# Gathering softmax probabilities by 4 wide matmuls and a block transpose in a decode-attention kernel

## The chip, the cores and the metric

The kernel runs on one core of one Trainium2 chip. The metric is the device time of one execution, in microseconds (us); lower is better. The kernel before took 1296.13 to 1296.85 us in its 25 executions.

## The reference, cut to what matters

One token is decoded for 4 sequences: a layer norm, attention over a cache of 8192 keys for each of 32 heads, a gated feed-forward layer, two residual sums. Nearly all bytes are the caches `k_cache` and `v_cache`, each (4, 32, 8192, 128) in bf16, 537 MB together.

```python
def _A_ref(x, k_cache, v_cache, wq, wo):
    q = (x @ wq).reshape(B, Sq, H, Dh).transpose(0, 2, 1, 3)
    scores = jnp.einsum("bhqd,bhkd->bhqk", q, k_cache) * (Dh ** -0.5)
    p = _softmax(scores, axis=-1)
    o = jnp.einsum("bhqk,bhkd->bhqd", p, v_cache)
    return o.transpose(0, 2, 1, 3).reshape(B, Sq, H * Dh) @ wo
```

## The kernel before

K and V come in loads of 4 MB (two heads each) into a ring of 4 slots of SBUF. VectorE (DVE) transposes K blocks, TensorE (PE) makes the scores, and eight heads form a group: 16 groups in all. At the end of a group ScalarE (ACT) takes the exponential of 128 x 512 scores into `E_sb`. There the keys run along the columns; this kernel's value matmuls take them from the partitions (weights of 128 x 32 out of `PTz`). The kernel before moves them with 64 small matmuls per group: each takes 32 columns of `E_sb` as the stationary operand and a selection matrix `Sel` as the moving one. Two ACT copies then place the result in `PTz`, the stationary operand of the value matmuls.

```python
        def chain_pt(g):
            def f(e):
                mm = None
                for rr in range(16):
                    for a in range(4):
                        mm = e.matmul(bP[g % 2][32 * a:32 * (a + 1), 32 * rr:32 * rr + 32],
                                      E_sb[:, 32 * rr:32 * rr + 32], Sel[:, a, :], start=True, stop=True,
                                      tile_position=(0, 32 * a))
                return mm
            pt_of[g] = P("pe", f, [exp_of[g], c_sel] + list(ptc_of.get(g - 2, ())))
            # ... two ACT copies: PTz <- bP[g % 2], strided, lists them in ptc_of[g]
```

The scores of one head and its value product, 16 matmuls each, are the bulk of PE's program (cut):

```python
        def pe_score(s):
            # ...
                for v in range(4):
                    l0 = LQ0 + (t * 4 + v) * 32 - 4 * hh
                    for j in range(4):
                        # ... rhs = 512 columns of kT
                        mm = e.matmul(bS[g % 2][32 * j:32 * (j + 1), :], Lq[:, l0:l0 + 32], rhs,
                                      start=(s % GS == 0 and v == 0), stop=(s % GS == GS - 1 and v == 3),
                                      tile_position=(0, 32 * j))
```

Each `matmul` becomes two PE instructions, a weight load and a matmul (5827 of each in the trace of the kernel before).

## Time and profile before

Median 1296.3 us.

| | before |
|---|---|
| span of the profiled execution | 1294.5 us |
| read from HBM | 550.8 MB |
| busy: DVE, PE, ACT | 48%, 39%, 4% |
| PE matmuls (and as many weight loads) | 5827 |

First, from the page of the kernel before: busy time by engine, the row of the DMA engines' busy tenths in 40 slices, and the DMA queues (packets, MB, share of the 16 engines' span).

```profile
PE 499.5 (39%) x5827; PEld 193.4 (15%) x5827; DVE 625.4 (48%) x641; ACT 46.1 (4%) x102; POOL 10.6 (1%) x22
DMA  9999999999999999999999999999999999999998
q1 hardware_dynamic: 26016, 550.78, 99.5%
q8 instruction: 45, 0.74, 0.2%
q14 instruction: 7, 0.06, 0.0%
```

No compute engine is near full (DVE, the fullest, is busy 48%); the DMA engines are, at 80% or more in every slice and 90% or more in all but the last. Queue 8 brings instructions, 45 packets in the span, each of 16384 bytes in the trace. The loads are queue 1.

Second, the table by stage (start and end, length, busy time of each engine, PE clock, DMA share, GB/s), two of its rows.

```profile
140.00:400.00 260.00, 102.68 (x1187) 40.02 (x1187) 125.68 (x125) 8.54 (x20) 0.00 (x0) 0.60 1.00 430
400.00:800.00 400.00, 149.21 (x1666) 55.28 (x1665) 195.44 (x194) 10.67 (x25) 0.00 (x0) 0.60 1.00 431
```

In these stages the DMA engines moved 430 to 431 GB/s with a share of 1.00.

Third, groups of instructions that the change touches, and the largest one of DVE (busy us, mean ns of one | idle time just before them and its releaser).

```profile
L397 DVE STREAM_TRANSPOSE kT<-ring 128x1024 uint32<-128x1024 uint32 x512 | 587.9, 1209 | 578.8 <-DMA ring<-in_A_k_cache_dram 578.6
L506 ACT ACTIVATE PTz<-PS 64x512 bf16<-64x512 f32 x32 | 18.9, 592 | 16.5 <-PE PS L492 16.1
L492 PE MATMUL PS<-Sel,E_sb 128*32 128x32 bf16 x1024 | 11.0, 183 | 1.6 <-ACT E_sb L476 1.1
```

Fourth, the timeline at one group's end (start us, length us, engine, line, operation; idle before in brackets).

```profile
613.82 0.69 ACT L476 ACTIVATE E_sb<-PS,negm 128x512 bf16<-128x512 f32 x1
614.65 0.66 PE L492 MATMUL PS<-Sel,E_sb 128*32 128x32 bf16 x64
615.40 1.21 ACT L506 ACTIVATE PTz<-PS 64x512 bf16<-64x512 f32 x2 [0.81 <-PE PS L492]
619.57 9.13 DVE L397 STREAM_TRANSPOSE kT<-ring 128x1024 uint32<-128x1024 uint32 x8 [9.25 <-DMA ring<-in_A_k_cache_dram]
629.39 1.90 PE L439 MATMUL PS<-ring,PTz 128*32 128x512 bf16 x16 [2.73 <-DMA ring<-in_A_v_cache_dram]
```

The gather ends at 615.3 and `PTz` is ready at 616.6, but its first reader starts at 629.39, when its V load has landed. DVE is idle for 9.25 us until 619.57, when the next K load lands.

### The profile page before, as it was taken

The numbers are of one execution on the slowest core, as the hardware profiler recorded it, in microseconds if no ns is written. First come the engines' busy times: TensorE is split into PE (matmuls) and PEld (weight loads), VectorE is DVE, ScalarE is ACT, GpSimd is POOL, SyncE is SP. The second block draws the span as 40 slices with busy tenths as digits, with TensorE's granted clock in tenths as the row PEclk, the third lists the DMA queues.
The fourth block names the chain that finished last, engine by engine and source line by source line (L and its number), as shares of the span: only waits on it lengthen the run. The fifth ranks groups of instructions, "written<-read, shape, count | busy, mean of one in ns | idle before, by whom it ended". The sixth has DMA issues, their size and how long they took to land.

```text
span 1294.5 us, 12693 instructions
## 1 busy us (share of the span) xinstructions
PE 499.5 (39%) x5827; PEld 193.4 (15%) x5827; DVE 625.4 (48%) x641; ACT 46.1 (4%) x102; POOL 10.6 (1%) x22
## 2 busy tenths in 40 slices
PE   3444334335244244334334334343343343343436
PEld 1011111112011021111111111011110111111114
DVE  5964644535544544535535435445535446445300
ACT  2000000000000000000000000000000000000000
POOL 3000000000000000000000000000000000000000
PEclk9996565665565565565666665665665665656655
DMA  9999999999999999999999999999999999999998
GB/s 405 434 428 432 432 428 433 431 430 430 433 431 430 433 429 431 433 427 433 434 426 434 431 427 435 429 431 435 425 434 432 426 435 428 431 434 429 429 376 322
DMA packets 26076, 551.58 MB, mean 426 GB/s; under 512 B 2340, under 2 KB 8232, under 8 KB 9256
## 3 DMA queue, kind: packets, MB, share of 16 engines
q1 hardware_dynamic: 26016, 550.78, 99.5%
q8 instruction: 45, 0.74, 0.2%
q14 instruction: 7, 0.06, 0.0%
q10 hardware_dynamic: 8, 0.00, 0.0%
HBM read 550.77 MB, written 0.00 MB: 425 GB/s over the span
## 4 chain that ended last, share of the span: by engine, by line
DMA 81%; PE 12%; SPq 4%; DVE 3%; issue 0%
DMA ring<-in_A_v_cache_dram 79%; PE PS L439 7%; PE PS L415 4%; SPq L220 2%; DVE kT L397 2%; SPq L236 1%; DMA ring<-in_A_wq_dram 1%; DMA ring<-in_B_w_down_dram 1%; SPq L228 1%; SPq L256 0%; PE PS L330 0%; DVE Lq L374 0%; DVE ring L347 0%; PE PS L357 0%; PE PS L637 0%
## 5 line engine op out<-in xcount | busy, mean ns | idle before, releaser
L397 DVE STREAM_TRANSPOSE kT<-ring 128x1024 uint32<-128x1024 uint32 x512 | 587.9, 1209 | 578.8 <-DMA ring<-in_A_k_cache_dram 578.6
L415 PE MATMUL PS<-kT,Lq 128*32 128x512 bf16 x2048 | 241.6, 619 | 563.3 <-DVE kT L397 443.8
L439 PE MATMUL PS<-ring,PTz 128*32 128x512 bf16 x2048 | 215.0, 564 | 208.7 <-DMA ring<-in_A_v_cache_dram 208.3
L415 PEld LDWEIGHTS PS<-kT,Lq 128*32 128x32 bf16 x2048 | 69.4, 135 | 692.4 <-DVE kT L397 471.9
L439 PEld LDWEIGHTS PS<-ring,PTz 128*32 128x32 bf16 x2048 | 64.5, 127 | 326.4 <-DMA ring<-in_A_v_cache_dram 197.1
L474 ACT ACTIVATE negm<-PS 128x1 f32<-128x1 f32 x16 | 2.7, 171 | 1156.3 <-PE PS L470 1156.3
L511 DVE TENSOR_SCALAR Zs<-PS,rinv 128x512 f32<-128x512 f32 x16 | 11.6, 723 | 36.4 <-PE PS L439 36.4
L506 ACT ACTIVATE PTz<-PS 64x512 bf16<-64x512 f32 x32 | 18.9, 592 | 16.5 <-PE PS L492 16.1
L518 PE MATMUL PS<-SelZ,Zs 128*128 128x8 f32 x128 | 19.1, 276 | 0.9 <-DVE Zs L511 0.9
L518 PEld LDWEIGHTS PS<-SelZ,Zs 128*128 128x128 f32 x128 | 17.6, 213 | 10.6 <-issue 8.9
L453 DVE TENSOR_REDUCE mx<-PS 128x1 f32<-128x512 f32 x16 | 10.5, 658 | 5.4 <-PE PS L415 5.4
L492 PEld LDWEIGHTS PS<-Sel,E_sb 128*32 128x32 bf16 x1024 | 10.4, 96 | 8.3 <-ACT E_sb L476 7.1
L492 PE MATMUL PS<-Sel,E_sb 128*32 128x32 bf16 x1024 | 11.0, 183 | 1.6 <-ACT E_sb L476 1.1
L476 ACT ACTIVATE E_sb<-PS,negm 128x512 bf16<-128x512 f32 x16 | 11.0, 688 | 0.5
L481 PEld LDWEIGHTS PS<-sig,Gsum 128*128 128x128 f32 x32 | 7.8, 305 | 12.6 <-issue 12.6
L481 PE MATMUL PS<-sig,Gsum 128*128 128x1 f32 x32 | 9.2, 356 | 0.0
L470 PEld LDWEIGHTS PS<-onesf,rowx 1*128 1x128 f32 x32 | 7.3, 281 | 13.0 <-issue 13.0
L470 PE MATMUL PS<-onesf,rowx 1*128 1x1 f32 x32 | 8.6, 336 | 0.0
L523 DVE CAST OT<-PS 128x8 bf16<-128x8 f32 x16 | 2.1, 132 | 11.6 <-PE PS L518 11.6
L347 DVE CAST ring<-PS 128x512 bf16<-128x512 f32 x4 | 2.5, 683 | 10.0 <-PE PS L330 10.0
L485 DVE RECIPROCAL rinv<-PS 128x1 f32<-128x1 f32 x16 | 2.1, 130 | 9.3 <-PE PS L481 9.3
L330 PE MATMUL PS<-ring,xnT 128*32 128x512 bf16 x32 | 3.6, 629 | 6.6 <-DMA ring<-in_A_wq_dram 6.6
(78 smaller groups left out, 81.3 us busy)
## 6 DMA issues: line engine op xcount, KB each, us to landing
ring<-in_A_k_cache_dram SPq DMA_DIRECT2D x64, 4096.0 KB, 29.7
ring<-in_A_v_cache_dram SPq DMA_DIRECT2D x63, 4096.0 KB, 34.0
ring<-in_A_wq_dram SPq DMA_DIRECT2D x1, 4096.0 KB, 12.3
kT<-in_A_wo_dram SPq DMA_DIRECT2D x8, 512.0 KB, 17.3
ring<-in_A_v_cache_dram SPq DMA_DIRECT2D x1, 2048.0 KB, 18.5
ring<-in_A_v_cache_dram SPq DMA_DIRECT2D x2, 1024.0 KB, 18.2
ring<-in_B_w_gate_dram SPq DMA_DIRECT2D x1, 1792.0 KB, 19.9
ring<-in_B_w_up_dram SPq DMA_DIRECT2D x1, 1792.0 KB, 23.5
```

The costliest lines, as they stand in the source:

```text
L220: return [(lambda e: e.dma_start(wo_v[:, HW * t:HW * t + HW, :], A_wo.rearrange("(h p) f -> p h f", p=128)[:, HW * t:HW * t + HW, :]).then ...
L228: return e.dma_start(ringv(slot)[:, c0:c1], kv_src(t, A_v_cache)[:, c0:c1]).then_inc(s_piece[i], 16)
L236: return e.dma_start(wd_v[:, t0:t1, :], B_w_down.rearrange("(t p) f -> p t f", p=128)[:, t0:t1, :]).then_inc(s_piece[3 + i], 16)
L397: return e.transpose(kT[:, buf, i * q:(i + 1) * q].bitcast(U32), ringv(src)[:, base + i * q:base + (i + 1) * q].bitcast(U32))
L415: mm = e.matmul(bS[g % 2][32 * j:32 * (j + 1), :], Lq[:, l0:l0 + 32], rhs, start=(s % GS == 0 and v == 0), stop=(s % GS == GS - 1 and v == 3),
L439: mm = e.matmul(bO[g % 2][32 * rq:32 * (rq + 1), :], PTz[:, g % 2, l0:l0 + 32], ringv(slot)[:, r0 * 128:(r0 + 4) * 128], start=(s % GS == ...
L470: p2_of[g] = P("pe", lambda e: e.matmul(bX[:, 0:1], rowx[0:1, :], onesf[0:1, 0:1], start=True, stop=True), [d2b_of[g], c_ones])
L481: L_of[g] = P("pe", lambda e: e.matmul(bX[:, 0:1], Gsum[:, :], sig[:, 0:1], start=True, stop=True), [exp_of[g], a1_of[g], d_g])
L492: mm = e.matmul(bP[g % 2][32 * a:32 * (a + 1), 32 * rr:32 * rr + 32], E_sb[:, 32 * rr:32 * rr + 32], Sel[:, a, :], start=True, stop=True, ...
L506: return e.activation(dst, src, ACT.Copy)
L511: z_of[g] = P("dve", lambda e: e.tensor_scalar(Zs[:, :], bO[g % 2][:, :], rinv[:, g % 2:g % 2 + 1], None, op0=ALU.mult), [pv_of[g * GS + G ...
L518: mm = e.matmul(bX[:, 256:264], Zs[:, 128 * r:128 * (r + 1)], SelZ[:, r, :], start=(r == 0), stop=(r == 3))
```

## The change

The intent is to take work from PE: 4 matmuls of 512 columns with `Sel` as the stationary operand gather whole rows of `E_sb`; ACT copies the result to SBUF; one DVE instruction is meant to transpose it in blocks of 32 x 32, which is what this layout needs; the two ACT copies then read from there. The gather now writes one PSUM tile (`bP[0]`) instead of two in turn, and waits for the copy of the group before. The diff, cut:

```diff
+        Ep = SB("Ep", [128, 512], BF16)
+        Et = SB("Et", [128, 512], BF16)
@@ chain_pt
-                for rr in range(16):
-                    for a in range(4):
-                        mm = e.matmul(bP[g % 2][32 * a:32 * (a + 1), 32 * rr:32 * rr + 32],
-                                      E_sb[:, 32 * rr:32 * rr + 32], Sel[:, a, :], start=True, stop=True,
-                                      tile_position=(0, 32 * a))
+                for a in range(4):
+                    mm = e.matmul(bP[0][32 * a:32 * (a + 1), :], Sel[:, a, :], E_sb[:, :], start=True, stop=True,
+                                  tile_position=(0, 32 * a))
                 return mm
-            pt_of[g] = P("pe", f, [exp_of[g], c_sel] + list(ptc_of.get(g - 2, ())))
+            pt_of[g] = P("pe", f, [exp_of[g], c_sel, epc_of.get(g - 1)])
+            epc_of[g] = P("act", lambda e: e.activation(Ep[:, :], bP[0][:, :], ACT.Copy), [pt_of[g], et_of.get(g - 1)])
+
+        def chain_et(g):
+            et_of[g] = P("dve", lambda e: e.transpose(Et[:, :], Ep[:, :]), [epc_of[g]] + list(ptc_of.get(g - 1, ())))
 # ... the two copies into PTz
-                    src = bP[g % 2][p0:p0 + 64, :].rearrange("p (q r m) -> p q m r", q=4, r=4)
+                    src = Et[p0:p0 + 64, :].rearrange("p (q r m) -> p q m r", q=4, r=4)
 # ... chain_et(g) stands on DVE just before the key transposes of step 8 g + 10
```

More of the change, by code (lines that the diff above doesn't have):

```diff
@@ L387, in bass_sequential_preLN__mha_block_cached__glu_gated_glu__decode_kernel @@
         mx_of, d2_of, exp_of, pt_of, ptc_of, L_of, d3_of = {}, {}, {}, {}, {}, {}, {}
-        z_of, ot_of, otc_of = {}, {}, {}
+        z_of, ot_of, otc_of, epc_of, et_of = {}, {}, {}, {}, {}
         def dve_T(s):
@@ L504, in fc @@
                                   [[2 * 4128, 64], [1024, 4], [32, 32], [1, 4]])
-                    src = bP[g % 2][p0:p0 + 64, :].rearrange("p (q r m) -> p q m r", q=4, r=4)
+                    src = Et[p0:p0 + 64, :].rearrange("p (q r m) -> p q m r", q=4, r=4)
                     return e.activation(dst, src, ACT.Copy)
-                ops.append(P("act", fc, [pt_of[g], zp] + last_pv))
+                ops.append(P("act", fc, [et_of[g], zp] + last_pv))
             ptc_of[g] = ops
@@ L530, in bass_sequential_preLN__mha_block_cached__glu_gated_glu__decode_kernel @@
         for s in range(NST + LAG - 2 + 4):
+            g = hook(s, 10)
+            if g is not None:
+                chain_et(g)
             tr = dve_T(s) if s < NST else iter(())
@@ L646, in bass_sequential_preLN__mha_block_cached__glu_gated_glu__decode_kernel @@
         p_o = P("pe", lambda e: e.matmul(bP[0][0:NB, 0:128], oT[:, :], ident[:, :], start=True, stop=True),
-                [d_o] + list(ptc_of[gl]) + list(ptc_of[gl - 1]))
+                [d_o, epc_of[gl]])
         o0 = P("dve", lambda e: e.tensor_copy(o_sb[:, :], bP[0][0:NB, 0:128]), [p_o])
```

## The prediction

> **What bounds the kernel now.** The DMA engines. The table by stage gives DMA share 1.00 and 430 to 431 GB/s from 140 to 1216 us. 550.8 MB are read; at 431 GB/s that alone is 1278 of the 1294.5 us span. [...]so no compute engine can speed up the middle. The chain that ended last is 79% V loads. VectorE works 48%; its key transposes (512, 1209 ns each) wait 579 us for K loads. PE works 39%, ACT 4%.
>
> **What the change does**, once for each of 16 groups:
> - removes 64 32-column matmuls with their weight loads: 0.66 to 0.74 us a group in the timeline;
> - adds 4 matmuls of 512 columns on 4 column tiles; four such value matmuls take about 0.65 us in the timeline, so PE gains next to no time, though it issues 1920 instructions fewer (2 x 60 x 16);
> - adds an ACT copy 128x512 out of PSUM: about 0.60 us (line 346, same shape, 602 ns), 9.6 us in all;
> - adds a DVE transpose 128x512 bf16: estimated 0.6 us, half of the 1209 ns of 1024 elements, 10 us in all;
> - moves the two PTz copies (592 ns each) behind these, reading SBUF instead of PSUM; I leave them at 0.6 us.
> So exp to PTz grows from about 2.7 to about 4.2 us a group.
>
> **Is that on the critical path?** In the middle, no. At the group near 611 us: exp ends 614.5, gather would end near 615.3, copy 616.0, transpose 616.7, PTz 618. DVE idles until the K load lands at 619.57, and the group's first value matmul starts only at 629.39, after its V load. About 3 us to spare; at 146 and 1162 us 2 to 3 us.
>
> In the first group DVE is delayed: its keys have already landed, so the transposes now starting at 73.2 us wait behind the new one for exp (76.6), gather and copy: about 5.5 us later, and K and V slots are released that much later (82.2 to about 87.7, 87.6 to about 91). But loads are then issued some 29 us before they land, so about 15 us of transfers are still queued; DMA won't run dry, and the delay is absorbed at the next K load (DVE idled 9.75 us before 91.98).
>
> In the last group PTz is written by about 1233.3 instead of 1232.4; the next value matmul waits for DMA until 1236.5. Tail unchanged.
>
> A small gain: 12693 instructions came with 0.74 MB on the instruction queue, so 1900 fewer save about 0.11 MB, about 0.25 us of DMA time, an estimate.
>
> **Predicted:** 1296.1 us, 8 in 10 between 1295.2 and 1297.0. Faster by over 2%: 0.5%; within 2%: 99%; slower: 0.5%.
>
> **What would show it.** DMA share still 1.00 at 430 to 431 GB/s in the middle, and 431 from 60 to 140 us; DVE and ACT busy up by about 10 us each, PE within 2 us; about 1890 instructions fewer; DVE's idle time before the key transposes down by about 10 us or somewhat more, with a new wait of about 5 us for ACT at the first group only; fewer instruction-queue bytes.
>
> **What would make it wrong.** The new transpose or copy taking several us; DVE waiting for ACT in every group beyond the K load, so that slot releases slip by more than the queued 15 us; a hole in the DMA row at the first group; a strided PTz copy much slower from SBUF.

The sum is 1296.3 less about 0.25 us, so about 1296.1; that the middle can't be sped up by a compute engine rests on the share of 1.00 and the 1278 us of loads alone. The 15 us of queued transfers are an estimate; the trace gives about as much: 29.7 us from issue to landing (K loads, median), less the 9.7 us from one landing to the next and the 5.5 us of delay.

## The result, and the profile after

Median 1295.22 us (4 runs, 1295.11 to 1295.36) against 1296.3 us before: 1.08 us less. The ratio of the fast runs is 0.9992, with an interval of 0.9975 to 1.0009: the same, by the 2% measure. The changed kernel, run again later beside the kernel before on another occasion, gave 1295.18 against 1296.34, so the 1.1 us is real although it is small. No execution of the one overlaps one of the other.

The same lines of the page, after:

```profile
PE 494.7 (38%) x4867; PEld 183.3 (14%) x4867; DVE 636.9 (49%) x657; ACT 70.7 (5%) x118; POOL 10.7 (1%) x22
DMA  9999999999999999999999999999999999999998
q1 hardware_dynamic: 26016, 550.78, 99.5%
q8 instruction: 38, 0.62, 0.2%
q14 instruction: 7, 0.06, 0.0%
```

The table by stage, after, the same two rows:

```profile
140.00:400.00 260.00, 99.96 (x943) 36.29 (x944) 128.81 (x130) 14.68 (x24) 0.00 (x0) 0.61 1.00 431
400.00:800.00 400.00, 148.38 (x1379) 53.34 (x1382) 200.17 (x201) 18.34 (x30) 0.00 (x0) 0.59 1.00 431
```

The loads are the same. PE has 960 matmuls and 960 weight loads less, and queue 8 fetched 38 blocks instead of 45. The groups, after:

```profile
L399 DVE STREAM_TRANSPOSE kT<-ring 128x1024 uint32<-128x1024 uint32 x512 | 587.9, 1209 | 480.9 <-DMA ring<-in_A_k_cache_dram 480.9
L502 DVE STREAM_TRANSPOSE Et<-Ep 128x512 bf16<-128x512 bf16 x16 | 11.4, 712 | 97.4 <-ACT Ep L498 97.4
L511 ACT ACTIVATE PTz<-Et 64x512 bf16<-64x512 bf16 x32 | 34.0, 1062 | 12.8 <-DVE Et L502 12.5
L498 ACT ACTIVATE Ep<-PS 128x512 bf16<-128x512 f32 x16 | 9.6, 597 | 11.3 <-PE PS L494 11.3
L494 PE MATMUL PS<-E_sb,Sel 128*32 128x512 bf16 x64 | 7.0, 429 | 1.9 <-ACT E_sb L478 1.3
```

DVE now "waits 97.4 us for ACT". That is no new delay: idle time is booked to the instruction that ends it. The idle time before the key transposes is 97.9 us less (578.8 to 480.9), and the new transpose stands in that gap. The timeline of the same group shows how:

```profile
615.07 0.40 PE L494 MATMUL PS<-E_sb,Sel 128*32 128x512 bf16 x4
615.52 0.60 ACT L498 ACTIVATE Ep<-PS 128x512 bf16<-128x512 f32 x1 [0.50 <-PE PS L494]
616.15 0.71 DVE L502 STREAM_TRANSPOSE Et<-Ep 128x512 bf16<-128x512 bf16 x1 [5.74 <-ACT Ep L498]
616.90 2.15 ACT L511 ACTIVATE PTz<-Et 64x512 bf16<-64x512 bf16 x2 [0.78 <-DVE Et L502]
619.68 9.13 DVE L399 STREAM_TRANSPOSE kT<-ring 128x1024 uint32<-128x1024 uint32 x8 [2.82 <-DMA ring<-in_A_k_cache_dram]
629.50 1.90 PE L441 MATMUL PS<-ring,PTz 128*32 128x512 bf16 x16 [2.72 <-DMA ring<-in_A_v_cache_dram]
```

The idle 9.25 us became 5.74 us, the transpose of 0.71 us, and 2.82 us: the key transposes still start when their load lands.

So the new work is hidden. Where do 1.08 us come from? Not steadily from everywhere: the K and V loads land now earlier, now at the same time. A load raises its semaphore 16 times, and the trace has the time of each rise. The profile counts 16 DMA engines, and the author reads each rise as one engine's share of the load having landed, so that the time from the first to the last of the 16 is how far the latest engine is behind the earliest. That reading is not shown: the trace has the 16 rises but does not name their engines. Worked out from the recorded rises, for the loads around each jump (a load is complete at its 16th rise):

```
load (order)   before: complete, first to 16th   after: complete, first to 16th   after - before
   24th           238.00     2.17                   237.97     2.17                  -0.03
   25th           248.77     3.21                   247.68     2.17                  -1.09
   30th           297.46     3.34                   296.42     2.36                  -1.04
   31st           307.18     3.34                   307.27     3.50                  +0.09
   49th           482.41     3.70                   482.38     3.80                  -0.04
   50th           493.30     4.87                   492.09     3.81                  -1.21
   60th           590.42     4.89                   589.22     3.83                  -1.20
   61st           600.13     4.90                   600.23     5.13                  +0.10
  123rd          1205.87     8.44                  1205.54     8.43                  -0.33
  124th          1216.73     9.59                  1215.25     8.43                  -1.48

start of every eighth packet on queue 8 (the 9th, 17th, 25th, 33rd, 41st)
   before    243.1   491.1   730.6   966.5   1214.5
   after     300.4   593.4   886.3  1179.3   (38 in all, no 41st)
```

Three things can be seen. The spread of the 16 rises grows from 2 us to over 8 us during the run (by the reading, some engines fall further and further behind), and what waits for a load starts after its last rise (63rd load of the kernel before: 16th rise at 619.55 us, key transposes at 619.57). The spread doesn't grow evenly but by jumps of 1.0 to 1.3 us, with smaller ones of up to 0.6 us between. And each large jump comes in the load in flight after the 9th, 17th, 25th, 33rd, 41st instruction block. The durations of these packets repeat with a period of eight as well (changed kernel, from the 3rd block: 1060, 1099, 1107, 1095, 1016, 1026, 1073, 1078 ns, then about the same again). In the late loads 7 of the 16 rises come within 1.2 us and the rest 5 us or more after the first.

**Theory A** (a hypothesis: the trace names the engine neither of a packet nor of a rise). PE's instruction blocks go to about half of the DMA engines in turn, one block to each in eight. A block holds up its engine's share of the loads by about 1.1 us (the packets listed above took 1.02 to 1.11 us). The time is set by the engine that is furthest behind, and it gets one more block at every eighth. The kernel before meets five such blocks, the changed one four: one step of about 1.1 us.

**Theory B.** The gain comes from the new route itself: less PE time or PSUM traffic, `PTz` read from SBUF, other waits.

**The plain share of bytes** (as predicted): 7 blocks of 16384 bytes are 0.115 MB, and at 431 GB/s that is about 0.3 us.

### The profile page after: what moved, and what is told of

Its sections match the earlier page's. It is cut to its first block, busy times and chain, and to the rows that moved or that the text cites. A ratio compares the mean times of both kernels' runs of the same rounds, so it can differ in the third digit from the quotient of the medians.

```text
span 1293.4 us, 10805 instructions
## 1 busy us (share of the span) xinstructions
PE 494.7 (38%) x4867; PEld 183.3 (14%) x4867; DVE 636.9 (49%) x657; ACT 70.7 (5%) x118; POOL 10.7 (1%) x22
## 4 chain that ended last, share of the span: by engine, by line
DMA 80%; PE 12%; SPq 4%; DVE 3%; issue 0%; ACT 0%
DMA ring<-in_A_v_cache_dram 76%; PE PS L441 7%; PE PS L417 4%; SPq L222 2%; DMA ring<-in_A_k_cache_dram 2%; DVE kT L399 2%; SPq L238 1%; DMA ring<-in_A_wq_dram 1%; DMA ring<-in_B_w_down_dram 1%; SPq L230 1%; SPq L258 0%; PE PS L332 0%; DVE Lq L376 0%; DVE ring L349 0%; PE PS L359 0%
## 5 line engine op out<-in xcount | busy, mean ns | idle before, releaser
L399 DVE STREAM_TRANSPOSE kT<-ring 128x1024 uint32<-128x1024 uint32 x512 | 587.9, 1209 | 480.9 <-DMA ring<-in_A_k_cache_dram 480.9
L502 DVE STREAM_TRANSPOSE Et<-Ep 128x512 bf16<-128x512 bf16 x16 | 11.4, 712 | 97.4 <-ACT Ep L498 97.4
L511 ACT ACTIVATE PTz<-Et 64x512 bf16<-64x512 bf16 x32 | 34.0, 1062 | 12.8 <-DVE Et L502 12.5
L498 ACT ACTIVATE Ep<-PS 128x512 bf16<-128x512 f32 x16 | 9.6, 597 | 11.3 <-PE PS L494 11.3
L494 PE MATMUL PS<-E_sb,Sel 128*32 128x512 bf16 x64 | 7.0, 429 | 1.9 <-ACT E_sb L478 1.3
## 6 DMA issues: line engine op xcount, KB each, us to landing
ring<-in_A_k_cache_dram SPq DMA_DIRECT2D x64, 4096.0 KB, 29.7
```

Of the source, the lines that this page charges most:

```text
L399: return e.transpose(kT[:, buf, i * q:(i + 1) * q].bitcast(U32), ringv(src)[:, base + i * q:base + (i + 1) * q].bitcast(U32))
L502: et_of[g] = P("dve", lambda e: e.transpose(Et[:, :], Ep[:, :]), [epc_of[g]] + list(ptc_of.get(g - 1, ())))
L511: return e.activation(dst, src, ACT.Copy)
```

## The experiments

All runs passed the comparison with the reference. That is weak evidence here: two kernels that were wrong passed as well (half of the scores left out; probabilities in a wrong order). With this data the comparison can't show a mistake in that part.

### The narrow gather back, with the new route kept

```diff
-                for a in range(4):
-                    mm = e.matmul(bP[0][32 * a:32 * (a + 1), :], Sel[:, a, :], E_sb[:, :], ...
+                for rr in range(16):
+                    for a in range(4):
+                        mm = e.matmul(bP[0][32 * a:32 * (a + 1), 32 * rr:32 * rr + 32], Sel[:, a, :],
+                                      E_sb[:, 32 * rr:32 * rr + 32], ...
```

> The changed kernel, but its gather cut back into 64 matmuls of 32 columns a group (the rows are still gathered, and copy, block transpose and PTz copies stay): 2 x 60 x 16 = 1920 PE instructions more. Theory A (the gain of 1.08 us is the 7 blocks of 16 KB of PE instructions that are no longer fetched; each block holds up one DMA engine for about 1.1 us, and the loads end with the engine that is furthest behind): 45 blocks again, and 1296.2 us, within 0.3. Theory B (the gain comes from the new route itself: PTz read from SBUF, another order of waits, less work in PSUM): 1295.2 us, within 0.2. The plain share of bytes (0.11 MB at 431 GB/s) says 1295.5.

Measured: 1296.48 us (before: 1296.26). Its page has 45 blocks again:

```profile
q8 instruction: 45, 0.74, 0.2%
```

With the copy, the transpose and the SBUF reads all in place, the gain is gone. Theory B falls as far as these go; the number of PE instructions, or PE's time in the gather, is left.

### The narrow gather twice, in the kernel before

```diff
-                for rr in range(16):
+                for rr in [i % 16 for i in range(32)]:
```

> The kernel before, each of its 64 gather matmuls issued twice: 2048 PE instructions more, about 0.7 us of PE time a group, off the critical path. Theory A: 53 blocks of PE instructions instead of 45, one more turn of eight, so about 1.1 to 1.6 us more than before: 1297.4 to 1297.9. Theory B (PE instructions cost nothing while PE has slack): 1296.3 us, within 0.2. The plain share of bytes: 1296.6.

Measured: 1298.12 us, 53 blocks, the 49th at 1231 us: one step more than before, of 1.86 us, a little more than expected, and far from the 0.3 us of the plain share of bytes.

```profile
q8 instruction: 53, 0.87, 0.3%
```

### PE time without many instructions

```diff
-                for a in range(4):
+                for a in [i % 4 for i in range(24)]:
```

> The changed kernel with its four wide gather matmuls done six times: about 3 us of PE time more a group, but only 640 instructions more, 2.5 blocks, 40 or 41 in all. Theory A by steps: 1295.2 to 1295.5. If it is PE's time in the gather that costs (and not its instructions), this adds ten times what the 64 narrow matmuls of e1 did (0.3 us a group for 1.26 us in all): well over 1297.

Measured: 1295.14 us, with 40 blocks. The page, and the group of gather matmuls, which has grown:

```profile
PE 514.3 (40%) x5187; PEld 191.4 (15%) x5187; DVE 636.6 (49%) x657; ACT 70.7 (5%) x118; POOL 10.6 (1%) x22
q8 instruction: 40, 0.66, 0.2%
L494 PE MATMUL PS<-E_sb,Sel 128*32 128x512 bf16 x384 | 24.9, 397 | 1.9 <-ACT E_sb L478 1.4
```

PE is busy 514.3 us here, more than in the kernel before (499.5), and the time is that of the changed kernel. So it is not PE's time.

### Half as narrow: a step or a slope?

```diff
+                for rr in range(8):
+                    for a in range(4):
+                        mm = e.matmul(bP[0][32 * a:32 * (a + 1), 64 * rr:64 * rr + 64], Sel[:, a, :],
+                                      E_sb[:, 64 * rr:64 * rr + 64], ...
```

> The changed kernel with its gather in 32 matmuls of 64 columns a group: 2 x 28 x 16 = 896 PE instructions more, 3.5 blocks, so 41 or 42 blocks. [...] If it goes by such steps: the 41st block is fetched in the last few us, when nearly all loads are in, so 1295.2 to 1295.5. If each block costs its share (1.26 us for 7 blocks): 1295.8.

Measured: 1296.30 us with 41 blocks, outside both expectations.

```profile
q8 instruction: 41, 0.67, 0.2%
```

The full step is there with one block more than the 40 of the last experiment. The expectation erred about the end: the 41st block was fetched at 1288.3 us, and the last piece of `w_down` was then still in flight. The waits of the last matmuls show it. First this run, then the changed kernel:

```profile
1288.36 0.70 PE L647 MATMUL PS<-hh_sb,ring 128*128 128x4 bf16 x20 [0.64 <-DMA ring<-in_B_w_down_dram]
1291.02 0.59 PE L647 MATMUL PS<-hh_sb,ring 128*128 128x4 bf16 x16 [1.96 <-DMA ring<-in_B_w_down_dram]
```

```profile
1288.23 1.26 PE L645 MATMUL PS<-hh_sb,ring 128*128 128x4 bf16 x31 [0.47 <-issue]
1290.15 0.59 PE L645 MATMUL PS<-hh_sb,ring 128*128 128x4 bf16 x16 [0.65 <-DMA ring<-in_B_w_down_dram]
```

The last 16 matmuls waited 1.96 us for their load instead of 0.65. In the recorded rises the piece before the last was complete at 1288.32 (changed kernel: 1288.76), and the last at 1290.97 (1290.10). Of the 16 rises of that last piece, 15 had come by 1289.66; only the 16th was 1.3 us later. One block, one late rise, one step, at the very end.

### One turn of eight less

```diff
-                for v in range(4):
+                for v in range(2):
                     # and stop=... v == 1: half of the score matmuls, a wrong result on purpose
```

> The changed kernel with half of its score matmuls left out (the result is wrong on purpose): 4 x 2 x 2 x 128 = 2048 PE instructions less, all loads and VectorE work unchanged. Theory A by steps: 30 blocks of PE instructions instead of 38, so the 33rd is never fetched and one more step of 1.1 to 1.3 us goes: 1293.7 to 1294.3. If the gain of the change was something in the gather's route: 1295.2, within 0.3, as before this edit.

Measured: 1293.57 us with 30 blocks, 1.6 us under the changed kernel of the same rounds (1295.18).

```profile
q8 instruction: 30, 0.49, 0.2%
```

The direction and the step hold; the time is 0.1 to 0.7 us lower than expected. The rises account for all of it: at the 127th load, near 1247 us, their spread is 6.60 us here and 8.31 us in that changed kernel, 1.7 us less. Why this step is larger than the others stays open.

The runs in order of their blocks, with the spread of the 16 rises at the 127th load (1246 to 1251 us, profiled execution):

| kernel | PE instruction blocks | of these 9th, 17th, ... | us, median | spread, us |
|---|---|---|---|---|
| half of the scores | 30 | 3 | 1293.57 | 6.60 |
| the changed kernel | 38 | 4 | 1295.22, 1295.18 | 8.74, 8.31 |
| wide gather six times | 40 | 4 | 1295.14 | 8.17 |
| gather in 32 | 41 | 5 | 1296.30 | 8.09 (41st block later) |
| the kernel before | 45 | 5 | 1296.3 | 9.69 |
| changed, gather in 64 | 45 | 5 | 1296.48 | 9.58 |
| before, gather twice | 53 | 6 | 1298.12 | 11.59 |

The time goes by the third column, not by the second: 38 and 40 are alike, 41 and 45 are alike. The steps are 1.1 to 1.9 us. The last column shows where they sit: but for the gather in 32, whose 41st block came after that load, the kernels differ in time by about as much as in spread.

### The same number of instructions on another engine

```diff
+        scr = SB("scr", [128, 2], BF16)
+        prev = c_mean
+        for i in range(2048):
+            prev = pool(lambda e: e.memset(scr[:, 0:1], 0.0), [prev])
```

> The changed kernel with 2048 one-column memsets on the otherwise idle POOL engine, after its set-up work: as many instructions more as the gather matmuls cost PE, but for another engine. If any engine's instruction bytes delay the loads as PE's do (theory A, widened): up to 1.9 us more, 1296.0 to 1297.2, depending on which DMA engines fetch them. If only PE's blocks of 16 KB fall on the DMA engines that are behind: 1295.2, within 0.3.

Measured: 1297.94 us, 2.7 us over the changed kernel, more than expected; so theory A has to be widened to other engines. The page:

```profile
q8 instruction: 38, 0.62, 0.2%
q14 instruction: 23, 0.19, 0.0%
```

PE's blocks stay at 38, and queue 14 has 16 packets more, of 8192 bytes. They were fetched about every 20 us up to 323 us. In the recorded rises the last one is 0.65 us later with each of these packets, until it is 11.2 us behind the first at 509 us (the 15th rise of that load comes at 3.4 us). By the reading of one rise for one engine, all of POOL's blocks fall to one engine; the trace does not name it. The last rise then stays there, while the other late rises fall back as in the changed kernel: at the load that completes near 1216 us the last rise comes 11.3 us after the first here and 8.4 us in the changed kernel. The difference, 2.9 us, is about the 2.7 us that the run lost. At 509 us the loads were 7.4 us later than in the changed kernel, and most of that never reached the end: what counts here is by how much the last rise is behind, whichever blocks made it late. The memsets keep POOL busy as well as being fetched, and this run does not part the two; the packets and the single late rise speak for the fetching.

### Is the transpose free, or did it just fit?

```diff
+            for _ in range(7):
+                t2_of[0] = P("dve", lambda e: e.transpose(Et2[:, :], Ep[:, :]), [epc_of[g], t2_of.get(0)])
```

> The changed kernel with the block transpose of every group done eight times (seven into a spare tile): about 5 us of VectorE time more a group, over the 2.8 us that it idled between the new transpose and the next key load. If VectorE is off the critical path by the depth of the load queue (some 15 us of transfers still queued), the keys of that group start 2 to 3 us late and the time stays 1295.2, within 0.3. If the new transpose was only free because it fitted the idle time, each of 15 groups adds its 2 to 3 us: 1325 to 1340 us.

Measured: 1295.03 us. The timeline of the same group:

```profile
616.32 5.19 DVE L504 STREAM_TRANSPOSE Et<-Ep 128x512 bf16<-128x512 bf16 x7 [5.85 <-ACT Ep L499]
621.55 0.71 DVE L505 STREAM_TRANSPOSE Et<-Ep 128x512 bf16<-128x512 bf16 x1
622.19 9.09 DVE L400 STREAM_TRANSPOSE kT<-ring 128x1024 uint32<-128x1024 uint32 x8
639.28 1.25 DVE L400 STREAM_TRANSPOSE kT<-ring 128x1024 uint32<-128x1024 uint32 x1 [7.31 <-DMA ring<-in_A_k_cache_dram]
```

The key transposes start at 622.19 instead of 619.68, 2.5 us late, and DVE is idle again before the next load. Nothing reaches the total: the queue of loads already issued covers it (K loads are issued a median of 29.7 us before they land, in the changed kernel). The prediction's claim about DVE holds with room to spare.

### Moving bytes to other DMA engines (no clear answer)

```diff
+        SHIFT = (30,)
# ... 24 KB of each row as before; then 8 KB of each row in 16 parts of 8 partitions:
+            if kind == "v" and t in SHIFT:
# ...
+                for i in range(16):
+                    def f(e, p=slice(8 * i, 8 * i + 8)):
+                        return e.dma_start(ringv(slot)[p, CW:TW], kv_src(t, A_v_cache)[p, CW:TW]).then_inc(sem, 16)
```

> The changed kernel, with 8 KB of each row of one V load (1 MB in all) carried by 16 transfers of 8 partitions each instead of by the one transfer of 128 partitions. In the trace 8 of the 16 completions of a load come up to 8.4 us after the other 8 by 1186 us. If a transfer of 8 partitions runs on 8 of the 16 DMA engines only, this moves about 2.4 us of work onto those 8 and as much off the others. If those are the ones that finish early: up to 2.4 us faster, 1292.8 to 1294.5. If they are the late ones: up to 2.4 us slower, 1296.5 to 1298. If the lag is not a matter of single DMA engines: 1295.2, or a little slower for 16 more issues.

Measured: 1302.67 us, 7.4 us slower, outside all three expectations. In the stretch in question the loads ran at 319 GB/s, against 431 otherwise:

```profile
660.00:680.00 20.00, 6.24 (x64) 2.00 (x64) 7.79 (x7) 0.00 (x0) 0.00 (x0) 0.53 1.01 319
```

That alone is about 5.2 us ((431 - 319) / 431 of 20 us). Why the stretch with the 16 small transfers was slower was not followed up, so the run can't say which engines are the late ones, nor that single engines are. A kernel that gives less work to the late engines was therefore not found.

### Two side questions about single instructions

`PTz` copies took 1062 ns instead of 592. Is it the 2-byte source?

```diff
-        Ep = SB("Ep", [128, 512], BF16)
-        Et = SB("Et", [128, 512], BF16)
+        Ep = SB("Ep", [128, 512], FP32)
+        Et = SB("Et", [128, 512], FP32)
```

> The changed kernel with Ep and Et in fp32 instead of bf16 (values the same). The PTz copies took 1062 ns from bf16 in SBUF against 592 ns from fp32 in PSUM with the same read pattern. If it is the 2-byte read in that pattern: about 600 ns here. If it is SBUF as the source: about 1062 ns. The block transpose took 712 ns for 512 bf16 elements against 1209 for 1024 of 4 bytes[...]. The time of the kernel: 1295.2, within 0.3, either way.

```profile
L511 ACT ACTIVATE PTz<-Et 64x512 bf16<-64x512 f32 x32 | 34.5, 1078 | 12.8 <-DVE Et L502 12.4
L502 DVE STREAM_TRANSPOSE Et<-Ep 128x512 f32<-128x512 f32 x16 | 11.4, 711 | 97.0 <-ACT Ep L498 97.0
```

It isn't: 1078 ns from fp32. The transpose takes 711 ns for 512 elements of 4 bytes and 712 ns for 512 of 2 bytes. The time of the kernel was 1295.25 us, as expected. The other reading, a source in SBUF with that stride, was tried with a read straight on (order of probabilities wrong):

```diff
-                    src = Et[p0:p0 + 64, :].rearrange("p (q r m) -> p q m r", q=4, r=4)
+                    src = Et[p0:p0 + 64, :].rearrange("p (q m r) -> p q m r", q=4, r=4)
```

> The changed kernel with the PTz copies reading Et straight on instead of every 32nd element (the result is wrong on purpose; destination pattern unchanged). If the 1062 ns of these copies come from the strided read of SBUF: about 600 ns here. If from SBUF as a source in any pattern: still about 1060 ns.

```profile
L511 ACT ACTIVATE PTz<-Et 64x512 bf16<-64x512 bf16 x32 | 20.1, 628 | 12.8 <-DVE Et L502 12.4
```

628 ns. So 434 ns of the 1062 go with the read of SBUF at a step of 32 elements; from PSUM the copies with the same read pattern took 592 ns. One look (a single run, state unknown) gave 1295.13 us, no gain over the changed kernel (1295.18): these copies are hidden either way.

### The changed kernel again

> The changed kernel as it is, timed on the same chip as the run before, so that the two can be compared: 1295.2, within 0.2.

Measured: 1295.18 us, against 1296.34 us for the kernel before in the same rounds. No version with a right result beat the changed kernel by more than the scatter.

## Why the prediction was right or wrong

The measured 1295.22 us lies in the range, by 0.02 us from its low edge. "Within 2%" was right. That the time fell inside the range is luck: single executions lie on both sides of the edge (1295.11 to 1295.36), and nearly all of the 0.9 us between it and the forecast of 1296.1 comes from one term of the sum, mis-sized by a factor of four.

- **DMA bounds the kernel, at 430 to 431 GB/s: right.** The stage rows after the change read 431 GB/s and 1.00 from 140 to 1216 us.
- **The new work is hidden in mid-run: right.** DVE kept 2.82 us of idle time in the group near 611 us (predicted about 3). The run with eight transposes (1295.03 us) shows that even overrunning it, by 2.5 us, cost nothing.
- **The first group delays DVE but not DMA: right.** DVE waited 4.84 us for ACT there (predicted about 5); slots came free at 88.0 and 91.7 us (predicted 87.7 and 91); the stretch from 60 to 140 us stayed at 431 GB/s; and 4.20 of the 9.75 us of idle time before the next K load were left.
- **The tail is unchanged: right for the copies.** `PTz` was ready at 1233.5 us, and its reader started at 1235.1 us, when its load had landed.
- **Durations: two of these four were off.** The copy took 597 ns (602 predicted) and the wide gather 0.38 to 0.64 us (0.65). The transpose took 712 ns (600 estimated by halving), and the `PTz` copies 1062 ns (592 kept). So ACT's busy time rose by 24.6 us, not 10, and exp to `PTz` took 4.8 us in most groups, not 4.2. None of it is on the path. PE's busy time fell by 4.8 us, where "within 2" was said.
- **DVE's idle time before the key transposes "down by about 10 us or somewhat more": wrong as a reading.** It fell by 97.9 us, because the wait for ACT in front of the new transpose took over that part of the same gaps in all groups.
- **"1900 fewer save about 0.11 MB, about 0.25 us of DMA time": the step that failed in size.** It spread 0.11 MB evenly over all engines at full rate. The runs showed that these 7 blocks, 0.115 MB, were worth 1.08 us, and that the price isn't per byte: it comes at every eighth block (when, by theory A, the engine that is furthest behind gets one more). Shown by the runs are the dependence on the number of PE instructions, the steps, and the growing spread of the rises. That each of eight DMA engines has its own place in the turn is argued from the period of eight and not shown engine by engine: the trace does not name the engine of a packet or of a rise.

## What to carry to other kernels

In this kernel, with a DMA share of 1.00, engine time in the gaps was free (PE busy 514.3 us instead of 494.7: 1295.14 us; seven transposes more a group: 1295.03 us), but instructions were not. PE's came in blocks of 16384 bytes on a DMA queue; the 33rd, 41st and 49th block each went with 1.1 to 1.9 us more, and the spread of the rises grew by about as much. Here 7 blocks were worth 1.1 of 1296 us. In a kernel whose profile looks like this one, try fewer instructions (one wide matmul for many narrow ones) and look at the instruction queues and at the spread of the 16 completions, not at busy shares. For the same reason, before counting a new "wait" as a loss, check whether an old wait at the same place has shrunk by as much.
